# Two feature maps put behind the first residual adds, and LN1 statistics and token sums placed at other products of the first key/value groups

## The chip, the cores and the metric

The kernel runs on one core of one Trainium2 chip. The metric is the device time of one execution in microseconds (us), as the median of several executions. TensorE, VectorE, ScalarE and GpSimd are called PE, DVE, ACT and POOL in the profile; PEld are the weight loads of PE, SP is the engine that issues most DMAs.

## The reference, cut to what matters

```python
def _A_ref(x, wqkv, wo):                       # x: layernorm of the input, 2048 tokens x 1024
    qkv = ...                                  # x @ wqkv, 32 heads of 32
    phi = lambda t: where(t > 0, t + 1, exp(t)) + 1e-6
    pq, pk = phi(q), phi(k)
    kv = einsum("bhsd,bhse->bhde", pk, v)      # summed over all tokens
    z = einsum("bhsd->bhd", pk)
    num = einsum("bhqd,bhde->bhqe", pq, kv)
    den = einsum("bhqd,bhd->bhq", pq, z)[..., None] + 1e-6
    return (num / den) @ wo
h  = x + _A_ref(layernorm(x), wqkv, wo)        # attention block
h2 = h + _B_ref(layernorm(h), ...)             # gated FFN, 3584 wide; not touched here
```

## The kernel before: the parts that matter

Tokens come in 16 tiles of 128. For each pair of tiles the kernel computes keys ("key group" p), then values for pair p+2 ("value group" p+2); later it computes queries in eight groups. Every such group makes a 2x2 block product from seven products instead of eight, as in Strassen's scheme. This needs sums of weights (`TWv`, `TWk`), sums of tokens (`Sx`, by `x_sums`) and copies of partial results from one PSUM bank to another (`ident_act`, on ACT; PSUM is the memory that the products are written to). A product is four matmuls of 128x512. At fixed points of a group ("hooks") other work is queued for DVE and ACT.

```python
def sgroup(pool, tok_major, X, SX, W, TW, e11, e12, e21, e22, name, hooks=(), isphi=True):
    ...
    prod(a, X(0, 0), W(0, 0), True, "P1")
    ident_act(bank(b), bank(a), ...)              # bank copy: P6 waits for it
    hook(1)
    prod(f, SX(2), TW(2), True, "P7")
    ident_act(s7, bank(f), ...)
    hook(2)
    prod(b, SX(1), TW(1), False, "P6")            # needs token sum 2 and the bank copy
    ident_act(bank(c), bank(b), ...)              # bank copy: P5 waits for it
    hook(3)
    prod(a, X(1, 0), W(1, 0), False, "P2")
    for f_ in e11(...): f_()                      # keys: exp on ACT, two DVE ops ("finish")
    hook(4)
    prod(c, SX(0), TW(0), False, "P5")
    ident_act(sc, bank(c), ...); s22 = e22(...); s22[0]()     # an add on DVE
    hook(5)
    prod(b, X(1, 1), TW(3), False, "P4")
    s21 = e21(...); s21[0]()                      # an add on DVE
    hook(6)
    for f_ in s22[1:2]: f_()                      # exp on ACT
    prod(c, SX(3), W(1, 1), False, "P3")
    s12 = list(e12(...)); s12.pop(0)()            # (keys and queries) exp on ACT
    pend[1] = list(s22[2:]) + s12 + list(s21[1:]) # the rest runs at hook 1 of the next group
    hook(7)
```

The statistics of LN1, the first layernorm, run on ACT for some tiles: a pass for the mean and a pass of squares, which can be split in two ("half-squares"). Both write sums into a slot `s1`, of which there are two, and a few tiny POOL operations follow before the tile can be normalized (DVE) and transposed into place by a DMA.

```python
def ln1_stats_act(st, split=False):
    k = len(ln1_a) % 2                            # slot: tiles 5, 6, 7, 9 take 0, 1, 0, 1
    ...
# first value pieces (cut): ... m6(); v_piece(3, 0); ...; q6(); v_piece(2, 1); ...
def k5():                                         # key group p
    if p + 2 < NP_: x_sums(p + 2, 0)
    if p == 0: m_, q0_, q_ = ln1_stats_act(B, True); m_(); sq.extend([q0_, q_])   # B = 2p + 7
    elif B < NST: late_q.pop(0)()
def k6():
    if p + 2 < NP_: x_sums(p + 2, 1)
def v2(): if sq: sq.pop(0)()                      # value group p + 2
def v3(): if sq: sq.pop(0)()
          # p == 0: x_sums(1); norm(6)     else: norm(2 * p + 6)
def v5(): norm(2 * p + 7)
          # B = 2p + 9: m_, q0_, q_ = ln1_stats_act(B, True); m_(); q0_(); late_q.append(q_)
```

The output projection follows the last query group. Each pass multiplies tile t-4 by `wo` into one of two bank pairs, makes the next numerators, divides them (DVE), adds the residual of tile t-4 (`a4_h`, DVE, reads the bank pair) and takes its LN2 statistics on ACT, whose unused output goes to a scratch tile that shares memory with the exponentials.

```python
flush()                                           # the pending rest of the last query group
for t in range(NE, NST + LAG + 1):                # NE = LAG = 4
    if LAG <= t < NST + LAG: a4_mm(t - LAG)
    if t < NST: a2_num(t); a2_div(t)              # division, then a DMA transpose of the tile
    if LAG <= t < NST + LAG: a4_h(t - LAG)
    if LAG + 1 <= t < TPP + LAG + 1: a4_norm(t - LAG - 1)
    if t in (5, 7, 18, 19): load_w_next()         # 512 KB of FFN weights
    ...
```

## Time and profile before

| | before |
|---|---|
| median of executions | 723.82 us (723.69 to 724.08) |
| span of the profiled execution | 722.1 us, granted clock 0.999 |
| PE busy | 714.2 us (99%) |

The page of the kernel before: its span, the busy time of the engines, and the chain of waits by engine.

```profile
span 722.1 us, 12877 instructions
...
PE 714.2 (99%) x4905; PEld 380.4 (53%) x4905; DVE 587.5 (81%) x1024; ACT 359.2 (50%) x623; POOL 108.4 (15%) x177
...
PE 90%; DVE 6%; issue 1%; ACT 1%; POOL 1%; DMA 0%; ACTq 0%; DVEq 0%
```

PE is the limit, and the little that is not PE does not show in "99%". It shows in the timeline of PE. The columns are start, duration, engine, line, operation, tiles, matrix size, shape, number of merged instructions and, in brackets, the idle time before and what ended it. The first stretch is that of the early groups.

```profile
30.25 1.03 PE L766 MATMUL ps<-RW,RWG 128*128 128x512 f16 x4
31.69 1.02 PE L766 MATMUL ps<-RW,RWG 128*128 128x512 f16 x4 [0.41 <-DVE RWG L984]
32.55 1.03 PE L766 MATMUL ps<-RAB 128*128 128x512 bf16 x4
33.63 1.04 PE L766 MATMUL ps<-RW,RWG 128*128 128x512 f16 x4
...
35.47 0.70 PE L766 MATMUL ps<-RE 128*32 128x33 bf16 x64
...
37.84 1.03 PE L766 MATMUL ps<-RC,RWG 128*128 128x512 f16 x4
39.39 1.04 PE L766 MATMUL ps<-RC,RWG 128*128 128x512 f16 x4 [0.53 <-ACT ps L771]
```

Read starts here, not durations: a product of four lasts 1.03 us in the records and yet the next one starts 0.87 us later when nothing is in the way (the Trainium skill, Perfetto Trace Analysis, section Tensor Engine Instruction, says that the profiler works out a matmul's end rather than seeing it; this trace can't show that, but its records do overlap, 1.03 against 0.87). So between 30.25 and 31.69 there are 1.44 us where 0.87 are needed: a gap of 0.58 us, although the bracket has only 0.41. "Gap" below is always this: start to start, less the back-to-back time of the matmuls between. 33.63 has 0.22 and 39.39 has 0.69.

Why 39.39 is late stands in the timeline of ACT. L804 are statistics, L771 is the bank copy for which PE waits.

```profile
36.95 1.06 ACT L804 ACTIVATE RXH<-RE 128x1024 bf16<-128x1024 bf16 x1 [1.58 <-DVE RXH L890]
37.91 0.18 ACT L804 ACTIVATION_READ_ACCUMULATOR RXH<-RE 128x1 f32 x1
38.13 0.63 ACT L804 ACTIVATE RXH<-RE 128x512 bf16<-128x512 bf16 x1
38.67 0.19 ACT L804 ACTIVATION_READ_ACCUMULATOR RXH<-RE 128x1 f32 x1
38.76 0.58 ACT L771 ACTIVATE ps<-ps 128x512 f32<-128x512 f32 x1
```

ACT had idled 1.58 us for norm 6 (L890), which still read the statistics slot that tile 9's mean was to overwrite, and the copy then stood behind mean and half-square.

The fourth gap is in the projection. First PE, then DVE, in the kernel before:

```profile
174.71 0.37 PE L766 MATMUL ps<-kvz,RAB 32*128 32x33 bf16 x32
175.79 3.63 PE L766 MATMUL ps<-RW,RE 128*128 128x512 bf16 x16 [0.70 <-DVE RXH L1229]
```

```profile
171.77 0.28 DVE L849 TENSOR_SCALAR RX<-RX 128x512 bf16<-128x512 bf16 x1
172.09 0.69 DVE L852 SCALAR_TENSOR_TENSOR RAB<-RXH,RX 128x512 bf16<-128x512 f32 x1
172.70 0.18 DVE L1200 TENSOR_SCALAR dtmp<-ps 128x32 f32<-128x32 f32 x1
...
174.52 1.22 DVE L1229 TENSOR_TENSOR RXH<-ps,RC 128x1024 bf16<-128x1024 f32 x1
```

The third projection tile starts 1.08 us after the numerators, 0.77 more than the 0.31 of later tiles: it waits for the first residual add (L1229), in front of which DVE works off the finishes of the last query group (L849 and L852).

### The profile page before, as it was taken

How to read it: one execution, taken by the hardware profiler on the slowest of the kernel's cores; microseconds unless marked ns; L12 is line 12 of the kernel's file. 1: busy time of each engine (PE TensorE's matmuls, PEld its weight loads, DVE VectorE, ACT ScalarE, POOL GpSimd, SP SyncE). 2: the span in 40 equal slices, each digit the busy share in tenths (PEclk: the TensorE clock that was granted, in tenths of full speed). 3: DMA queues.
4: the chain of work that ended last, by engine and by line, in shares of the span. 5: the costliest groups of instructions: out<-in, count | busy, mean ns of one | idle time of the engine just before them, and what ended most of it. 6: DMA issues, size and time to landing. Idle time of an engine off the chain costs nothing.

```text
span 722.1 us, 12877 instructions
## 1 busy us (share of the span) xinstructions
PE 714.2 (99%) x4905; PEld 380.4 (53%) x4905; DVE 587.5 (81%) x1024; ACT 359.2 (50%) x623; POOL 108.4 (15%) x177
## 2 busy tenths in 40 slices
PE   8999999999999999999999999999999999999998
PEld 3444444444444444444444558865555545447887
DVE  7878867898775889889988787887889877887984
ACT  4877666764842456677756111035455545423010
POOL 2311100000360103332321001310000000000331
PEclk9999999999999999999999999999999999999999
DMA  9643245023998797999999989993564572037996
GB/s 310 214 98 80 44 126 163 6 30 72 211 221 262 230 282 236 273 302 312 298 273 275 310 251 322 319 208 114 149 172 135 161 250 78 1 102 249 323 315 178
DMA packets 192989, 143.64 MB, mean 199 GB/s; under 512 B 51872, under 2 KB 170400, under 8 KB 192928
## 3 DMA queue, kind: packets, MB, share of 16 engines
q1 hardware_dynamic: 188224, 138.50, 65.3%
q0 software_dynamic: 4032, 3.67, 3.5%
q8 instruction: 38, 0.62, 0.3%
q10 hardware_dynamic: 672, 0.66, 0.3%
q14 instruction: 23, 0.19, 0.1%
HBM read 98.76 MB, written 32.51 MB: 182 GB/s over the span
## 4 chain that ended last, share of the span: by engine, by line
PE 90%; DVE 6%; issue 1%; ACT 1%; POOL 1%; DMA 0%; ACTq 0%; DVEq 0%
PE ps L766 90%; DVE RAB L852 1%; DVE RE L1205 1%; DVE st L780 1%; DVE RX L849 1%; POOL rstd L790 0%; DVE RW L959 0%; DMA RE<-in_A_x_dram 0%; DVE RC L959 0%; DVE RX L1065 0%; ACT RX L845 0%; ACT RXH L804 0%; DVE RXH L834 0%; DVE rden L1203 0%; ACT ps L771 0%
## 5 line engine op out<-in xcount | busy, mean ns | idle before, releaser
L771 ACT ACTIVATE ps<-ps 128x512 f32<-128x512 f32 (+1 forms) x192 | 108.8, 567 | 217.4 <-PE ps L766 207.1
L766 PE MATMUL ps<-RC,RO 128*128 128x512 f16 x616 | 143.0, 369 | 0.0
L766 PE MATMUL ps<-RH,RWG 128*128 128x512 bf16 x448 | 108.1, 379 | 0.0
L766 PEld LDWEIGHTS ps<-RC,RO 128*128 128x128 f16 x616 | 60.3, 98 | 63.5
L766 PE MATMUL ps<-RC,RWG 128*128 128x512 f16 x320 | 76.7, 379 | 0.5 <-ACT ps L771 0.5
L766 PEld LDWEIGHTS ps<-RH,RWG 128*128 128x128 bf16 x448 | 43.8, 98 | 46.9
L1447 DVE TENSOR_TENSOR RAB<-ps,RAB 128x512 bf16<-128x512 f32 x56 | 37.3, 686 | 31.3 <-PE ps L766 31.3
L766 PE MATMUL ps<-RH,RO 128*128 128x512 bf16 (+1 forms) x256 | 61.2, 379 | 0.0
L766 PE MATMUL ps<-RW,RE 128*128 128x512 bf16 x256 | 57.6, 380 | 0.7 <-DVE RXH L1229 0.7
L1647 POOL DMA_DIRECT2D out_dram<-RX x20 | 17.9, 1257 | 263.3 <-DVE RX L1638 221.0
L766 PE MATMUL ps<-RAB 128*128 128x512 bf16 (+2 forms) x270 | 57.1, 351 | 0.1
L766 PE MATMUL ps<-RW,RAB 128*128 128x256 f16 (+3 forms) x362 | 52.9, 301 | 0.0
L766 PEld LDWEIGHTS ps<-RC,RWG 128*128 128x128 bf16 (+1 forms) x320 | 30.1, 98 | 40.1 <-ACT ps L771 6.1
L771 ACT ACTIVATE RE<-ps 128x512 f32<-128x512 f32 (+1 forms) x64 | 31.5, 502 | 37.8 <-PE ps L766 37.8
L766 PEld LDWEIGHTS ps<-RW,RAB 128*128 128x128 f16 (+1 forms) x362 | 35.4, 98 | 14.5
L1638 DVE TENSOR_TENSOR RE<-ps,RE 128x512 f32<-128x512 f32 x44 | 30.2, 687 | 14.3 <-PE ps L766 13.8
L771 ACT ACTIVATE RAB<-ps 128x512 bf16<-128x512 f32 x56 | 33.3, 595 | 16.5 <-PE ps L766 16.2
L1331 DVE TENSOR_TENSOR RO<-RWG 128x1024 f16<-128x1024 bf16 x54 | 36.9, 684 | 4.9 <-DMA RWG<-in_B_W_up_dram 4.9
L766 PEld LDWEIGHTS ps<-RH,RO 128*128 128x128 f16 (+1 forms) x256 | 24.4, 98 | 29.9 <-ACT RX L771 1.5
L1442 ACT ACTIVATE RAB<-RAB 128x1024 bf16<-128x1024 bf16 x28 | 29.5, 1055 | 19.5 <-DVE RAB L1433 19.0
L766 PEld LDWEIGHTS ps<-RW,RE 128*128 128x128 bf16 x256 | 24.0, 98 | 28.7 <-DVE RXH L1229 1.2
L766 PEld LDWEIGHTS ps<-RAB 128*128 128x128 bf16 (+1 forms) x270 | 26.0, 98 | 24.4 <-ACT RAB L908 1.0
(163 smaller groups left out, 1169.6 us busy)
## 6 DMA issues: line engine op xcount, KB each, us to landing
RWG<-in_B_W_gate_dram SPq DMA_DIRECT2D x28, 512.0 KB, 6.2
RWG<-in_B_W_up_dram SPq DMA_DIRECT2D x28, 512.0 KB, 5.2
RW<-l_scr SPq DMA_DIRECT2D x20, 448.0 KB, 5.6
RW<-in_B_W_down_dram SPq DMA_DIRECT2D x14, 512.0 KB, 5.2
t_scr<-RW SPq DMA_DIRECT2D x14, 512.0 KB, 4.9
l_scr<-RX SPq DMA_DIRECT2D x7, 1024.0 KB, 6.5
RE<-l_scr SPq DMA_DIRECT2D x15, 448.0 KB, 4.9
RE<-in_A_x_dram SPq DMA_DIRECT2D x23, 256.0 KB, 3.8
```

The source lines that it names most:

```text
L766: lambda e: e.matmul(out_ap, lhsT, rhs, start=start, stop=stop, skip_group_check=skip),
L771: PL.add("act", lambda e: e.activation(out=dst, in_=src, func=func), reads=reads, writes=writes, name=name)
L780: PL.add("dve", lambda e: e.bn_stats(out=st6[:, k, c * 6:(c + 1) * 6], in_=src_full[:, c * BCH:(c + 1) * BCH]), reads=[src_chunk_bufs[c]], ...
L849: PL.add("dve", lambda e: e.tensor_scalar(out=Et[:, k, :], in0=Et[:, k, :], scalar1=1.0, scalar2=1e-6, op0=ALU.min, op1=ALU.add), reads=[] ...
L852: PL.add("dve", lambda e: e.scalar_tensor_tensor(out=dst_ap, in0=src, scalar=C1, in1=Et[:, k, :], op0=ALU.add, op1=ALU.max), reads=[src_bu ...
L1205: PL.add("dve", lambda e: e.tensor_tensor(out=osb[:, k, :].rearrange("p (g h e) -> p g h e", h=HPG, e=Dh), in0=nv[:, :, :, 0:Dh], in1=rden ...
L1331: PL.add(eng, lambda e: e.tensor_tensor(out=tb(j, u), in0=f0(u), in1=f1(u), op=ALU.subtract), reads=[B_w[i + x] for x in r] + ([B_T[k + x] ...
L1442: PL.add("act", lambda e: e.activation(out=d, in_=d, func=ACTF.Relu), reads=[], writes=db, name=name)
L1447: PL.add("dve", lambda e: e.tensor_tensor(out=d, in0=bank(b), in1=d, op=ALU.mult), reads=[B_bank[b]], writes=[db], name=name)
L1638: PL.add(eng, lambda e: e.tensor_tensor(out=dst, in0=in0, in1=in1, op=op), reads=reads, writes=writes, name=name)
L1647: PL.add("pool", lambda e: e.dma_start(dst, src, accum_op=ALU.add), reads=[bsrc], writes=[B_hscr[st]], slot=sl, name="acc_%d_%d" % (st, dh))
```

## The change

Its intent: take DVE work from in front of the first residual adds, and place statistics and sums of the first groups so that PE's products are not kept waiting. The core of the diff:

```diff
-        s1 = sb("s1", [P, 2, 4], f32)
+        s1 = sb("s1", [P, 3, 4], f32)             # and k = len(ln1_a) % 3
 # sgroup, last query group
+            if last:
+                pend[1] = s12 + [s21[1]]
+                return [s22[2], s21[2]]           # two finishes, run by the caller
 # a4_h: scratch of the LN2 statistics
-            for f_ in act_stats(src, [B_hs[hs]], junk, B_junk, ...):
+            for f_ in act_stats(src, [B_hs[hs]], xn[:, st % NXN, :], B_xn[st % NXN], ...):
 # first value pieces
-        m6()
         v_piece(3, 0)
+        m6()
 ...
-        q6()
         v_piece(2, 1)
+        q6()
 ...
-        twv.pop(0)()                              # one of four value-weight sums; now in k6
 # key group p
+            def k4():
+                if p == 0: x_sums(2, 0)
             def k5():
+                if p == 0: x_sums(2, 1)
+                elif p + 2 < NP_: x_sums(p + 2, 0)
                 ...
-                elif B < NST: late_q.pop(0)()
+                while p > 0 and late_q: late_q.pop(0)()
             def k6():
+                if p == 0: twv.pop(0)()
 # value group p + 2
-                def v2(): ... sq.pop(0)()         # tile 7's half-squares now at v3 and v4
 # v3: norm(6) ahead of x_sums(1) when p == 0; from p = 1 on the first half-square of
 #     tile 2p + 9 moves from v5 to v3
                 def v5():
                     norm(2 * p + 7)
+                    if p == 0:
+                        m_, q0_, q_ = ln1_stats_act(9, True)
+                        m_(); late_q.extend([q0_, q_])
 # projection loop
                 a4_h(t - LAG)
+                run(late_phi, 1)
```

The scratch had to move with the late finishes: the old one shares memory with exponentials that they still read (so the code says).

More of the change, by code (lines that the diff above doesn't have):

```diff
@@ L321, in bass_sequential_preLN__linear_attn_block__glu_gated_reglu__prompt_kernel @@
         Et = RX[:, 0:NPH * NW].rearrange("p (a b) -> p a b", a=NPH)
-        ajunk = RX[:, 0:D]
         btmp = RX[:, NPH * NW:(NPH + 4) * NW].bitcast(f32).rearrange("p (a b) -> p a b", a=2)
@@ L427, in bass_sequential_preLN__linear_attn_block__glu_gated_reglu__prompt_kernel @@
         B_s2 = [bufs("s2_%d_" % i, 5) for i in range(2)]
-        B_s1 = [bufs("s1_%d_" % i, 4) for i in range(2)]
-        B_junk = _Buf("junk")
+        B_s1 = [bufs("s1_%d_" % i, 4) for i in range(3)]
         B_hnT = bufs("hnT_", TPP)
@@ L506, in bass_sequential_preLN__linear_attn_block__glu_gated_reglu__prompt_kernel @@
             b_.over = B_xn + B_hs
-        B_junk.over = B_E
         for b_ in flat(B_lsum):
-            b_.over = B_E + B_bt + [B_TWq[2], B_junk]
+            b_.over = B_E + B_bt + [B_TWq[2]]
         for b_ in B_hres + B_ds:
@@ L512, in bass_sequential_preLN__linear_attn_block__glu_gated_reglu__prompt_kernel @@
         for b_ in B_outst:
-            b_.over = B_E + B_bt + [B_TWq[2], B_junk]
+            b_.over = B_E + B_bt + [B_TWq[2]]
         for b_ in B_hnE:
@@ L880, in ln1_stats_act @@
             i = st % NX1
-            k = len(ln1_a) % 2
+            k = len(ln1_a) % 3
             ln1_a[st] = k
@@ L993, in x_sums, with sgroup @@
             add(3, xb(1, 0), s(1), ALU.subtract, [B_Sx[1][p]] + bx(1, 0))
-        def sgroup(pool, tok_major, X, SX, W, TW, e11, e12, e21, e22, name, hooks=(), isphi=True):
+        def sgroup(pool, tok_major, X, SX, W, TW, e11, e12, e21, e22, name, hooks=(), isphi=True, last=False):
             hooks = dict(hooks)
@@ L1157, in pl @@
                 return lambda b, bb: phi_steps(b, bb, d, db, "q_%d_%d" % (r, ct))
-            sgroup(A_POOL[r], False, X, SX, W, TW, pl(0, 0), pl(0, 1),
+            return sgroup(A_POOL[r], False, X, SX, W, TW, pl(0, 0), pl(0, 1),
                    add_phi(*dst(1, 0), "q_%d_%d" % (r, ct)),
-                   add_phi(*dst(1, 1), "q_%d_%d" % (r, ct)), "q%d%d" % (r, ct), hooks)
+                   add_phi(*dst(1, 1), "q_%d_%d" % (r, ct)), "q%d%d" % (r, ct), hooks,
+                   last=(r, ct) == (1, NG // 2 - 1))
         def kvacc(st):
@@ L1240, in a4_h @@
             src = hsb[:, hs, :]
-            junk = ajunk
-            for f_ in act_stats(src, [B_hs[hs]], junk, B_junk, s2[:, ks, 0:4], B_s2[ks], "ln2_%d" % st):
+            for f_ in act_stats(src, [B_hs[hs]], xn[:, st % NXN, :], B_xn[st % NXN], s2[:, ks, 0:4], B_s2[ks],
+                                "ln2_%d" % st):
                 f_()
@@ L1934, in bass_sequential_preLN__linear_attn_block__glu_gated_reglu__prompt_kernel @@
         m6, q6 = ln1_stats_act(6)
+        v_piece(3, 0)
         m6()
-        v_piece(3, 0)
         ln1_norm(5)
@@ L1939, in bass_sequential_preLN__linear_attn_block__glu_gated_reglu__prompt_kernel @@
         twk.pop(0)()
+        v_piece(2, 1)
         q6()
-        v_piece(2, 1)
         twv.pop(0)()
         twk.pop(0)()
-        twv.pop(0)()
         twv.pop(0)()
@@ L1960, in k1 @@
                     twq.pop(0)()
+            def k4():
+                if p == 0:
+                    x_sums(2, 0)
             def k5():
-                if p + 2 < NP_:
+                if p == 0:
+                    x_sums(2, 1)
+                elif p + 2 < NP_:
                     x_sums(p + 2, 0)
@@ L1968, in k5 @@
                     sq.extend([q0_, q_])
-                elif B < NST:
+                while p > 0 and late_q:
                     late_q.pop(0)()
             def k6():
-                if p + 2 < NP_:
+                if p == 0:
+                    twv.pop(0)()
+                elif p + 2 < NP_:
                     x_sums(p + 2, 1)
-            return {1: k1, 5: k5, 6: k6}, sq
+            return {1: k1, 4: k4, 5: k5, 6: k6}, sq
         def norm(st):
@@ L1998, in bass_sequential_preLN__linear_attn_block__glu_gated_reglu__prompt_kernel, with v3 @@
             if p + 2 < NP_:
-                def v2(sq=sq):
-                    if sq:
-                        sq.pop(0)()
-                def v3(p=p, sq=sq):
+                late = []
+                def v3(p=p, sq=sq, late=late):
                     if sq:
@@ L2006, in v3, with v4, v5 @@
                     if p == 0:
+                        norm(6)
                         x_sums(1)
-                        norm(6)
                     else:
                         norm(2 * p + 6)
-                def v5(p=p):
+                        if 2 * p + 9 < NST:
+                            m_, q0_, q_ = ln1_stats_act(2 * p + 9, True)
+                            q0_()
+                            late += [m_, q_]
+                def v4(sq=sq):
+                    if sq:
+                        sq.pop(0)()
+                def v5(p=p, late=late):
                     norm(2 * p + 7)
-                    B = 2 * p + 9
-                    if B < NST:
-                        m_, q0_, q_ = ln1_stats_act(B, True)
-                        m_()
-                        q0_()
-                        late_q.append(q_)
+                    if p == 0:
+                        m_, q0_, q_ = ln1_stats_act(9, True)
+                        m_()
+                        late_q.extend([q0_, q_])
+                    elif late:
+                        late[0]()
+                        late_q.append(late[1])
                 def v6(p=p, nq=nq):
@@ L2024, in v6 @@
                         twq.pop(0)()
-                v_group(p + 2, {2: v2, 3: v3, 5: v5, 6: v6})
+                v_group(p + 2, {3: v3, 4: v4, 5: v5, 6: v6})
         assert not twq and not twv and not twk
@@ L2038, in bass_sequential_preLN__linear_attn_block__glu_gated_reglu__prompt_kernel @@
                     hooks[6] = lambda t=ct: a2_num(t)
-                q_group(r, ct, hooks)
+                late_phi = q_group(r, ct, hooks)
                 if r == 1:
```

## The prediction

> **What bounds the kernel.** TensorE: matmuls busy 714.2 of 722.1 us (99%, page), granted clock 0.999, 90% of the chain of waits. The Trainium skill (Perfetto Trace Analysis, Identifying the Most-Contended Engine) warns that pipelined matmul busy time judges badly, so I measured in the timeline from matmul start to matmul start. A product of four 128x512 matmuls takes 0.87 us back to back. Beyond that, and 0.1 us per change of shape, four gaps lie where the change acts:
>
> - 31.69 us: 0.58 us, product 6 (P6) of value group 2: its token sum (VectorE, to 31.54) and bank copy (ScalarE, to 31.46) are late.
> - 33.63: 0.22 us, P5 there: its bank copy (32.98) stands behind a half-square of LN1 statistics (32.37).
> - 39.39: 0.69 us, P6 of key group 1: its bank copy (38.76) stands behind tile 9's mean (36.95, held until norm 6 by a shared statistics slot) and half-square (38.13).
> - 175.79: 0.86 us (0.77 net): the third output-projection tile waits for the first residual add (VectorE, 174.52 to 175.74), which reads the same banks.
>
> Sum 2.26 of 724 us. After 218 us no gap exceeds 0.25.
>
> **What the change does.**
>
> (a) The last query group's two feature-map finishes (0.92 us each) leave VectorE's queue ahead of the first residual add and run behind the first and second. VectorE runs without a pause from 163 to 178, so tile 4's division starts when its matmuls end (about 171.3) instead of 172.70, and the first add ends about 174.3, before 174.95 where its product could start. Later tiles have VectorE slack (idle 1.41 and 0.82). Gain 0.77.
>
> (b) The last value-weight sum (1.13 us) moves behind key group 0's feature maps, token sums of pair 2 one product earlier. The first finish starts near 27.6 instead of 28.21, the second token sum ends near 30.3 instead of 31.54. Then the bank copy rules; the exponentials ahead of it start 0.3 us earlier, so P6 starts near 31.2, 0.1 us late. Gain 0.45.
>
> (c) Tile 7's half-squares sit one product later, behind the copy; but the exponential ahead now waits for an add behind three token sums. Gain 0.15 to 0.2.
>
> (d) A third statistics slot frees tile 9's mean from norm 6; its half-squares go to the next group. Mean done near 36.4, copy on time near 37.4. Gain 0.65 to 0.7.
>
> (e) The new LN2 scratch tile: off the chain, zero.
>
> Against this, VectorE's backlog moves about 1 us later at 36 to 44 us, and two half-squares precede two exponentials in key group 1: a new gap of 0 to 0.2 us near value group 3.
>
> 2.26 less 0.2 to 0.3 left or new: 2.0 us. What follows is TensorE bound, so it should reach the end whole.
>
> **Predicted: 721.8 us, 8 in 10 within 721.2 to 723.0.** Faster by over 2%: 1%; within 2%: 98%; slower by over 2%: 1%.
>
> **Right or wrong shows in** the timeline: third output-projection tile 0.3 us after the division matmuls' start, not 1.08; key group 1's P6 without its 1.02 us weight-load wait on ScalarE; value group 2's P6 gap at most 0.2; TensorE's 0.7 us wait for the residual add gone.
>
> **Wrong if** the VectorE backlog holds token sums of pairs 1 or 3 (value group 3 waits over 0.3 us), if transposes of tiles 6 and 7 land later, if the late finishes delay later adds, or if the end hangs on a DMA that does not move along.

## The result, and the profile after

| | before | changed | |
|---|---|---|---|
| median | 723.86 us (723.69 to 724.08, 4 runs) | 722.61 us (722.40 to 723.35, 4 runs) | ratio 0.9984, 95% interval 0.9967 to 1.0002 |
| the same again, other chip | 724.49 us (9 runs) | 722.91 us (5 runs) | ratio 0.9981, 0.9967 to 0.9994 |
| span of the profiled execution | 722.1 us | 721.0 us; again 720.8 us | |

A ratio is the mean time of one kernel's fast runs over that of the other's of the same rounds, so not quite the ratio of the medians beside it. All runs told here are fast but one single run, whose state is unknown; their clocks lie between 0.999 and 1.0. The medians differ by 1.25 us, 0.17%. The first interval still includes 1, the second just does not: the gain is real by the second, and its size is loose. The page of the changed kernel:

```profile
span 721.0 us, 12872 instructions
...
PE 714.9 (99%) x4905; PEld 380.3 (53%) x4905; DVE 588.1 (82%) x1024; ACT 358.2 (50%) x623; POOL 110.7 (15%) x177
...
PE 94%; DVE 2%; DMA 2%; issue 1%; ACT 1%; POOL 0%; SPq 0%; DVEq 0%; ACTq 0%
```

The busy times do not tell that it is faster. PE's share of the chain went from 90 to 94%. The timeline of PE in the early groups (these line numbers are smaller by three in the changed kernel, so L763 is the L766 of before; of the later ones, the residual add L1229 is L1230):

```profile
30.20 2.06 PE L763 MATMUL ps<-RW,RWG 128*128 128x512 f16 x8
32.10 1.03 PE L763 MATMUL ps<-RAB 128*128 128x512 bf16 x4
33.07 1.04 PE L763 MATMUL ps<-RW,RWG 128*128 128x512 f16 x4
...
34.91 0.83 PE L763 MATMUL ps<-RE 128*32 128x33 bf16 x64
...
37.41 1.94 PE L763 MATMUL ps<-RC,RWG 128*128 128x512 f16 x8
...
43.59 1.03 PE L763 MATMUL ps<-RW,RWG 128*128 128x512 f16 x4
44.93 1.02 PE L763 MATMUL ps<-RW,RWG 128*128 128x512 f16 x4 [0.31 <-DVE RWG L981]
```

The three gaps have shrunk: P7 and P6 of value group 2 are now merged into one line of eight (0.16 us is left inside), P5 at 33.07 has 0.12, and in key group 1 P7 and P6 are one line too (nothing over the usual 0.04). But there are two new ones. The 64 small matmuls of the first key/value accumulation last 0.83 instead of 0.70, with a pause of 0.23 us in their middle (they follow each other faster than the spacing I reckon with, so of the pause 0.13 us are lost: the next product starts 0.76 us after the first of them, not 0.64), and at 44.93, P6 of value group 3, there are 0.48 us where before there were 0.04. What ACT and what DVE do ahead of 44.93:

```profile
41.69 0.62 ACT L801 ACTIVATE RXH<-RE 128x512 bf16<-128x512 bf16 x1
...
42.44 0.63 ACT L801 ACTIVATE RXH<-RE 128x512 bf16<-128x512 bf16 x1
...
43.06 0.61 ACT L842 ACTIVATE RX<-RX 128x512 bf16<-128x512 f32 x1
43.58 0.58 ACT L842 ACTIVATE RX<-ps 128x512 bf16<-128x512 f32 x1
44.06 0.59 ACT L768 ACTIVATE ps<-ps 128x512 f32<-128x512 f32 x1
```

```profile
31.30 1.22 DVE L956 TENSOR_TENSOR RW<-RAB,RW 128x2048 f16<-128x2048 bf16 x1
...
42.96 0.43 DVE L981 TENSOR_TENSOR RWG<-RAB 128x512 f16<-128x512 bf16 x1 [0.45 <-DMA RAB<-RXH]
...
44.35 0.42 DVE L981 TENSOR_TENSOR RWG<-RWG,RAB 128x512 f16<-128x512 f16 x1
```

The bank copy (L768) ends at 44.65, behind two half-squares (L801) and two exponentials. The token sum that P6 needs ends later still, at 44.77, because DVE stood 0.45 us for the transpose of tile 7. Which of them is the cause cannot be read from one trace. The 1.22 us weight sum (L956) is the piece that moved into DVE's queue here.

The projection, PE and DVE:

```profile
174.18 0.37 PE L763 MATMUL ps<-kvz,RAB 32*128 32x33 bf16 x32
174.49 3.63 PE L763 MATMUL ps<-RW,RE 128*128 128x512 bf16 x16
...
201.24 0.37 PE L763 MATMUL ps<-kvz,RAB 32*128 32x33 bf16 x32
201.80 3.61 PE L763 MATMUL ps<-RW,RE 128*128 128x512 bf16 x16 [0.19 <-DMA RE<-RE]
```

```profile
170.88 0.19 DVE L1201 TENSOR_SCALAR dtmp<-ps 128x32 f32<-128x32 f32 x1 [0.49 <-PE ps L763]
...
172.70 1.22 DVE L1230 TENSOR_TENSOR RXH<-ps,RC 128x1024 bf16<-128x1024 f32 x1
173.84 0.28 DVE L846 TENSOR_SCALAR RX<-RX 128x512 bf16<-128x512 bf16 x1
```

The third tile starts 0.31 us after the numerators, like all others: the gap is gone. DVE now waits for PE at 170.88, the add runs at 172.70, the first late finish (L846) after it. But at 201.80 the tenth tile starts 0.56 us after its numerators, 0.26 more than usual, for a DMA: the transposed tile landed at 201.7.

The stages, from the start of one matmul to the start of another (the same ones in all kernels, numbered in PE's order: 32, 361, 1301, 1471, 1901). Stage 1 is the value pieces and the early groups, stage 2 most of the rest of keys, values and queries, stage 3 the last query group and the first projection tiles, stage 4 most of the projection. From the end of stage 4 to the end of the span, which is nearly all FFN, it took 510.4 us in every trace of the tables.

| us | stage 1 | stage 2 | stage 3 | stage 4 |
|---|---|---|---|---|
| before | 43.48 | 107.15 | 17.52 | 34.34 |
| changed | 43.04 | 107.28 | 16.76 | 34.59 |
| changed, again | 42.78 | 107.25 | 16.75 | 34.53 |

Stage 3 gave what was forecast. Stage 1 gave 0.4 to 0.7 where 1.2 were gained at the three gaps, and stages 2 and 4 cost 0.1 and 0.2 to 0.25. Ahead of stage 1, where the change has no part, the traces differ as well: stage 1 starts at 9.16 us before, at 8.93 and 9.09 in the two of the changed kernel. So 0.23 and 0.07 us of the shorter spans are not the change's.

### The profile page after: what moved, and what is told of

Its sections match the earlier page's. It is cut to its first block, busy times and chain, and to the rows that moved or that the text cites. A ratio compares the mean times of both kernels' runs of the same rounds, so it can differ in the third digit from the quotient of the medians.

```text
span 721.0 us, 12872 instructions
## 1 busy us (share of the span) xinstructions
PE 714.9 (99%) x4905; PEld 380.3 (53%) x4905; DVE 588.1 (82%) x1024; ACT 358.2 (50%) x623; POOL 110.7 (15%) x177
## 4 chain that ended last, share of the span: by engine, by line
PE 94%; DVE 2%; DMA 2%; issue 1%; ACT 1%; POOL 0%; SPq 0%; DVEq 0%; ACTq 0%
PE ps L763 94%; DMA RE<-RE 1%; DMA RAB<-RXH 1%; DVE RWG L981 0%; DMA RE<-in_A_x_dram 0%; ACT RXH L801 0%; PE ps L902 0%; DVE RX L1065 0%; DVE RE L1639 0%; DVE st L777 0%; DVE RXH L1230 0%; DVE RE L1126 0%; ACT RXH L1256 0%; DVE RW L956 0%; DVE RX L846 0%
## 5 line engine op out<-in xcount | busy, mean ns | idle before, releaser
L768 ACT ACTIVATE ps<-ps 128x512 f32<-128x512 f32 (+1 forms) x192 | 108.9, 567 | 221.5 <-PE ps L763 214.7
L763 PE MATMUL ps<-RC,RO 128*128 128x512 f16 x616 | 143.0, 369 | 0.0
L763 PE MATMUL ps<-RH,RWG 128*128 128x512 bf16 x448 | 108.1, 379 | 0.0
L763 PEld LDWEIGHTS ps<-RC,RO 128*128 128x128 f16 x616 | 60.3, 98 | 63.5
L763 PE MATMUL ps<-RC,RWG 128*128 128x512 f16 x320 | 76.8, 379 | 0.0
L763 PEld LDWEIGHTS ps<-RH,RWG 128*128 128x128 bf16 x448 | 43.8, 98 | 46.9
L763 PE MATMUL ps<-RH,RO 128*128 128x512 bf16 (+1 forms) x256 | 61.2, 379 | 0.0
L763 PE MATMUL ps<-RW,RE 128*128 128x512 bf16 x256 | 57.6, 379 | 0.2 <-DMA RE<-RE 0.2
L763 PE MATMUL ps<-RAB 128*128 128x512 bf16 (+2 forms) x270 | 57.1, 351 | 0.1
L763 PE MATMUL ps<-RW,RAB 128*128 128x256 f16 (+3 forms) x362 | 52.9, 301 | 0.0
L763 PEld LDWEIGHTS ps<-RC,RWG 128*128 128x128 bf16 (+1 forms) x320 | 30.0, 98 | 39.8 <-ACT ps L768 5.8
L768 ACT ACTIVATE RE<-ps 128x512 f32<-128x512 f32 (+1 forms) x64 | 31.5, 503 | 37.8 <-PE ps L763 37.8
L763 PEld LDWEIGHTS ps<-RW,RAB 128*128 128x128 f16 (+1 forms) x362 | 35.3, 98 | 14.5
L768 ACT ACTIVATE RAB<-ps 128x512 bf16<-128x512 f32 x56 | 33.3, 594 | 16.9 <-PE ps L763 16.5
L763 PEld LDWEIGHTS ps<-RH,RO 128*128 128x128 f16 (+1 forms) x256 | 24.4, 98 | 29.9 <-ACT RX L768 1.5
L1434 DVE TENSOR_TENSOR RAB<-ps,RE 128x512 bf16<-128x512 f32 x56 | 37.2, 685 | 2.2 <-PE ps L763 1.9
L763 PEld LDWEIGHTS ps<-RAB 128*128 128x128 bf16 (+1 forms) x270 | 26.0, 98 | 24.4 <-ACT RAB L905 1.1
```

The costliest lines, as they stand in the source:

```text
L763: lambda e: e.matmul(out_ap, lhsT, rhs, start=start, stop=stop, skip_group_check=skip),
L768: PL.add("act", lambda e: e.activation(out=dst, in_=src, func=func), reads=reads, writes=writes, name=name)
L1434: PL.add("dve", lambda e: e.tensor_tensor(out=d, in0=src, in1=ftmp[:, u, :], op=ALU.add), reads=[bsrc, B_s5[u]], writes=[db], name=name)
```

## The experiments

Twelve runs, on four chips, each batch beside runs of the kernel before on its own chip. Four of the traces that the stages are read from lack 56 of 4905 matmul records; I matched the rest by their order. My theory was that each gap acts by itself, that gains and new gaps add up, and that the new gap at 44.93 comes from DVE's longer queue through the late transpose. Rivals: the new gaps are chance of one execution; the half-squares on ACT make them; the early gain is given back later.

### late_only, front_only: the two halves of the change

`late_only` is the kernel before with the late finishes and the new scratch; `front_only` is the changed kernel without them.

```diff
 # late_only, against before
+            if last: pend[1] = s12 + [s21[1]]; return [s22[2], s21[2]]
+                run(late_phi, 1)                  # after a4_h; and scratch xn[:, st % NXN, :]
 # front_only, against the changed kernel: these three edits taken out, the scratch left
```

Expected of `late_only`:

> Part (a) alone on the kernel before: the two late feature-map finishes with the new LN2 scratch tile. Theory: the parts add up, and this one removes only the gap in front of the third output-projection tile (0.86 to 0.09 us), so 0.77 us: 723.1 us, and the three early gaps (0.58, 0.22, 0.69 us) stay as in the kernel before. Rival: the gap is given back later (the finishes delay tiles 5 to 7, or the end hangs on something else), then the matmul starts after 190 us, or the total, move less than 0.5 us.

Expected of `front_only`:

> The whole change without part (a). Theory: the three early gaps shrink from 1.49 to about 0.3 us, but the change opens new ones in the same stage: 0.4 to 0.5 us at product 6 of value group 3 (its token sum waits for tile 7's transpose, which VectorE's backlog sends off late) and 0.1 to 0.2 us inside the first kv accumulation; net gain 0.4 to 0.6 us, 723.3 us; the gap at 175 us stays at 0.86. Rival: the new gap at value group 3 was a chance lateness of one transfer in one execution; then it is under 0.1 us here and the gain is about 1.0 us.

| | time (before 723.76) | ratio | stage 1 | stage 2 | stage 3 | stage 4 |
|---|---|---|---|---|---|---|
| late_only | 723.39 us | 0.9996 (0.9984 to 1.0009) | 43.60 | 107.15 | 16.75 | 34.40 |
| front_only | 723.47 us | 0.9997 (0.9984 to 1.0009) | 42.70 | 107.25 | 17.52 | 34.36 |

Stage 3 moves by 0.77 us with the late finishes and by nothing without them. That settles part (a). The time of `late_only` moved only 0.37 us; in its trace stage 4 took 0.06 more and its early stage had a gap of 0.80 us of another kind, told below. The three early gaps did not stay as expected either (0.03, 0.38 and 0.44 us instead of 0.58, 0.22 and 0.69; more under `slot_late`). So its expected total was missed. In `front_only` the new gap at P6 of value group 3 came back with 0.25 us instead of 0.48, and the pause in the first accumulation with 0.23. So they are not chance, but half of the first was.

### slot_only, slot_late: one line, and one line with part (a)

```diff
-        s1 = sb("s1", [P, 2, 4], f32)
+        s1 = sb("s1", [P, 3, 4], f32)             # and % 3; slot_late adds the edits of late_only
```

> The kernel before with three LN1 statistics slots instead of two, nothing else. Theory: tile 9's mean no longer waits for norm 6 and both its mean and its half-square end by 37.2 us, so the bank copy of key group 1 is on time: the 0.69 us gap is gone, the 0.58 and 0.22 us gaps stay, and no new gap over 0.1 us comes at value group 3 (its token sum would end 0.1 to 0.2 us before it is needed): 723.2 us, a larger gain than all of the early part of the change. Rival: any kernel in which TensorE runs ahead here meets the late transpose of tile 7, so value group 3 waits 0.4 us or more here too and the gain is under 0.4 us.

> Part (a) and the third statistics slot on the kernel before, nothing else. Theory: gains add, 0.77 and 0.69: 722.4 us, the same as or 0.1 to 0.3 us under the whole change, although it leaves the gaps of 0.58 and 0.22 us in value group 2. Rival: the reorderings of sums and statistics pay on balance, then this is at least 0.4 us slower than the whole change (723.0 us).

| | time (before 723.76) | ratio | stage 1 | stage 2 | stage 3 | stage 4 |
|---|---|---|---|---|---|---|
| slot_only | 723.45 us | 0.9996 (0.9982 to 1.0009) | 43.70 | 107.16 | 17.52 | 34.37 |
| slot_late | 722.83 us | 0.9989 (0.9976 to 1.0001) | 42.79 | 107.16 | 16.75 | 34.73 |

In both traces the 0.69 us gap of key group 1 is gone, and value group 3 has no gap over 0.04 us: the third slot alone takes the first away and opens no second. The gain in time, 0.31 us, was half of what was expected.

Both expectations said that the gaps of 0.58 and 0.22 us in value group 2 would stay. They did not. PE in `slot_late`:

```profile
30.67 1.93 PE L763 MATMUL ps<-RW,RWG 128*128 128x512 f16 x8
...
33.68 1.04 PE L763 MATMUL ps<-RW,RWG 128*128 128x512 f16 x4 [0.22 <-ACT ps L768]
```

P7 and P6 are one line (0.03 us), and P5 has 0.38; `slot_only` and `late_only` have the same. Nothing in these kernels mends P6. PE came to P7 at 30.67, 31.29 and 31.02 us, late by gaps further ahead, where it came at 30.25 in the kernel before; the token sum ended at 31.39, 31.96 and 31.69, against 31.54 there, in time for a PE that is late. So value group 2 lost 0.41 us in these three traces, not 0.80: the gap of 0.58 us was seen only where PE came early (there, and as 0.63 in `tw_back`, at 30.35), and gaps do not simply add up.

The two traces also say why one profile proves little here: the code of stage 1 is the same in both, and stage 1 differs by 0.9 us, through gaps of 0.61 and 0.68 us at 18 and 26 us in `slot_only` against one of 0.40 at 18 in `slot_late`. `slot_late` has the worst stage 4 of these four, with 0.26 us at the tenth tile and 0.15 at the ninth. Whether it equals the whole change is not settled: 0.9989 against 0.9984 and 0.9981 on other chips, inside the intervals.

### after_again, q0_back, tw_half, w_early: which new gap has which cause

`after_again` is the changed kernel unedited. The others each undo or mend one thing in it:

```diff
 # q0_back: tile 9's first half-square back in value group 2
-                        m_(); late_q.extend([q0_, q_])
+                        m_(); q0_(); late_q.append(q_)
 # tw_half: the moved weight sum in two halves, the first ahead of the first finish
+            def k3():
+                if p == 0: tw4.pop(0)()           # half the rows; k6 runs the other half
 # w_early: FFN weight loads ahead of the projection loop
+        load_w_next(); load_w_next()
-            if t in (5, 7, 18, 19):
+            if t in (18, 19):
```

> The changed kernel once more, unedited, to tell chance from cause. Theory: the new gaps of its first profile come from its order and return: at product 6 of value group 3 (0.48 us then) at least 0.2 us, inside the first kv accumulation 0.2 to 0.25 us; the wait of the projection for a transposed tile near 202 us (0.26 us beyond the usual 0.09) may move between 0 and 0.3 us, because its transfer takes 3.3 to 5 us. Rival: they were chance, and under 0.1 us here. Time 722.4 to 722.9 us.

> The changed kernel with tile 9's first half-square back in value group 2, where ScalarE idles 1.4 us. Theory: at product 6 of value group 3 ScalarE's copy comes about 0.6 us earlier, but the gap there stays at 0.3 to 0.5 us, because VectorE's token sum, which waits for tile 7's transpose, ends last; no gain on its own (0 to 0.1 us). Rival: ScalarE's two half-squares in key group 1 make the gap; then it is under 0.1 us and the gain 0.4 us.

> The changed kernel with the moved weight sum cut into two halves: the first fills VectorE's 0.78 us pause before the first feature-map finish (about 26.8 to 27.4 us), the second stays behind. Theory: VectorE's backlog shrinks by about 0.55 us: the gap in the first kv accumulation (0.24) goes, norms 6 and 7 come 0.5 us earlier, tile 7's transpose lands 0.3 to 0.5 us earlier, and the gap at product 6 of value group 3 falls from 0.48 to about 0.25 us, where ScalarE's copy is then last: gain 0.4 us, 722.2 us. Rival: the transposes are held by their own queue, not by VectorE, and land when they did: only the 0.24 us go.

> The changed kernel with the first two FFN weight loads (512 KB each) issued before the projection loop instead of in it (there they are issued near 183 and 192 us, between transposes). Theory: in the projection the transposes of the output tiles 6 to 9 land 0.5 to 2 us earlier, each with over 1 us to spare, and no projection tile waits for one: the gap near 202 us falls to 0.09 us; gain 0.2 to 0.3 us if that gap is there without the edit. Rival: the transposes slow each other, not the loads; then landing times and the gap stay as they are.

Gaps in us; the last two columns are the transpose of the tenth tile of the projection from issue to landing, and PE's gap before that tile beyond the usual 0.09.

| | time (before 724.49) | value group 3, P6 | pause, first accumulation | transpose, tenth tile | gap, tenth tile |
|---|---|---|---|---|---|
| after_again | 722.91 us | 0.25 | 0.23 | 5.0 | 0.19 |
| q0_back | 722.64 us | 0.04 | 0.24 | 4.8 | 0.09 |
| tw_half | 722.32 us | 0.26 | none | 3.4 | none |
| w_early | 722.81 us | 0.26 | 0.23 | 3.1 | none |

Ratios to before were 0.9981, 0.9979, 0.9975 and 0.9979, all with intervals of about 0.0013 either way, so the times do not part these kernels; the gaps do.

The gap at value group 3 was where I erred. I expected it to stay in `q0_back`, and it went. The trace of `q0_back`, PE first (P7 and P6 are one line of eight), then ACT:

```profile
43.97 1.93 PE L763 MATMUL ps<-RW,RWG 128*128 128x512 f16 x8
```

```profile
42.08 0.62 ACT L801 ACTIVATE RXH<-RE 128x512 bf16<-128x512 bf16 x1
...
42.94 0.63 ACT L842 ACTIVATE RX<-RX 128x512 bf16<-128x512 f32 x1
43.48 0.58 ACT L842 ACTIVATE RX<-ps 128x512 bf16<-128x512 f32 x1
44.23 0.58 ACT L768 ACTIVATE ps<-ps 128x512 f32<-128x512 f32 x1 [0.18 <-PE ps L763]
```

With one half-square ahead of the exponentials, the bank copy waits for PE and not PE for it. So 0.25 us of this gap belongs to the half-square that the change moved into key group 1. PE came to this group 0.27 us later here than in `after_again`, held by a gap of 0.81 us at 18 us, and that alone could have hidden the gap. `best1` below settles it: PE comes 0.14 us earlier than in `after_again`, and with the half-square back there is still only 0.03. The other 0.2 in the first profile came on top, in an execution where tile 7's transpose landed at 42.9; where DVE did not have to wait for it (`after_again`, 42.5) the gap was 0.25. `m6_again`, told below, repeats the larger gap: the transpose landed at 43.4, DVE stood 0.42 us for it, and P6 had 0.47.

`tw_half` shows that the pause in the first accumulation is the moved weight sum: with half of it in DVE's idle time it is gone. (The gap at value group 3, which was to fall from 0.48 to 0.25, says nothing here: `after_again` has 0.25 too.) `w_early` shows the loads' part in the projection: without them between the transposes, the eighth, ninth and tenth tile landed 3.0, 3.7 and 4.1 us ahead of their products, against 1.9, 0.5 and 0.1 us in `after_again`; in `best1`, with the same edit, it was 2.7, 3.6 and 4.1. In the traces with the loads in place the tenth transpose took either 3.1 to 3.4 us or 4.6 to 5.0 us; only in the second case, and only with part (a) in, did PE wait over 0.05 us for it (0.06 to 0.43 us). `tw_half` and `m6_old` had no wait with the loads in place, so for the wait itself the two traces with the loads moved are few.

### best1, tw_back, m6_old

`best1` has all three repairs. `tw_back` undoes the move of the weight sum, `m6_old` that of tile 6's statistics in the first value pieces.

```diff
 # tw_back
+        twv.pop(0)()                              # before v_piece(3, 1), and none in k6
 # m6_old
+        m6()
         v_piece(3, 0)
-        m6()
 ...
+        q6()
         v_piece(2, 1)
-        q6()
```

> The changed kernel with the three repairs that the runs so far point to, together: tile 9's first half-square back in value group 2, the moved weight sum cut in two halves, and the first two FFN weight loads ahead of the projection loop. Theory: each takes away a gap of its own, and they add up: at product 6 of value group 3 from 0.25 to under 0.1 us, in the first kv accumulation from 0.23 to 0, near 202 us to 0.09; together 0.45 to 0.7 us under the changed kernel. Rival: with those gaps gone TensorE runs into the next wait in the same places and less than 0.3 us is left.

> The changed kernel with the last value-weight sum back ahead of key group 0's feature maps, the token sums left at their new products. Theory: the gap at product 6 of value group 2 (0.16 us) grows to 0.5 to 0.7 us, because the first finish and the adds behind it, and with them ScalarE's exponentials and its bank copy, come 0.6 us later; the gap of 0.23 us in the first kv accumulation goes, for VectorE's queue is shorter there. Net loss 0.2 to 0.4 us in the early stage against the changed kernel. Rival: the earlier token sums alone keep product 6 on time; then its gap stays under 0.2 us and the kernel gains 0.2 us.

> The changed kernel with tile 6's two statistics passes back ahead of the value copies in the first value pieces. Theory: where the load of tile 6's tokens lands late (21 us and more instead of 20) ScalarE waits in the mean, its value copies and the bank copy of key group 0 come late, and TensorE has a gap of 0.5 to 0.8 us at product 6 of key group 0 near 25 us, as two of the four profiles with the old order had (0.80, 0.68 us; the other two none) and none of the new order over 0.2. Then the gap at product 6 of value group 2 closes. On time 0 to 0.4 us slower. Rival: the old order is no worse; that gap is under 0.2 us although the load lands after 21 us.

| | time (before 723.93) | ratio | stage 1 | stage 2 | stage 3 | stage 4 |
|---|---|---|---|---|---|---|
| best1 | 722.49 us (722.34 to 722.55) | 0.9978 (0.9965 to 0.9990) | 42.45 | 107.53 | 16.75 | 34.35 |
| tw_back | 722.83 us | 0.9984 (0.9972 to 0.9997) | 43.09 | 107.25 | 16.76 | 34.80 |
| m6_old | 723.95 us (722.76 to 724.42) | 1.0001 (0.9987 to 1.0014) | 42.68 | 107.56 | 16.76 | 34.35 |

In `best1` all three are gone; its stage 1 is the shortest of all, its stage 4 as short as any with part (a). Its stage 2 has 0.28 us at one product near 104 us, which `q0_back` and `m6_old` have too and the changed kernel does not; I did not find out why. In time it lies 0.0003 to 0.0006 under the changed kernel in ratio, 0.2 to 0.4 us, on another chip and inside the intervals: better than the changed kernel is not shown, and the 0.45 to 0.7 us expected were missed.

In `tw_back` PE's timeline has the gap back at P6 of value group 2, now with ACT's copy as the one waited for:

```profile
30.35 1.03 PE L763 MATMUL ps<-RW,RWG 128*128 128x512 f16 x4
31.84 1.04 PE L763 MATMUL ps<-RW,RWG 128*128 128x512 f16 x4 [0.47 <-ACT ps L768]
```

That is 0.63 us against 0.16, and the pause in the first accumulation is gone, as expected. So, in an execution in which PE comes as early as here, moving the weight sum gains 0.47 and costs 0.13, and moving the token sums alone would not have done. (Its stage 4 is the longest: 0.43 us at the tenth tile, the chance of this execution.)

`m6_old` is the surprise: an edit that only swaps statistics and copies in the first value pieces leaves four of five executions 1.1 to 1.7 us slower than the fifth, on which its profile fell, and slower than all of `best1` and `tw_back` on the same chip. What may lie behind it is seen in `late_only`, which has the old order. ACT, then PE:

```profile
21.59 1.06 ACT L801 ACTIVATE RXH<-RE 128x1024 bf16<-128x1024 bf16 x1 [1.14 <-DMA RE<-in_A_x_dram]
...
25.12 0.60 ACT L768 ACTIVATE ps<-ps 128x512 f32<-128x512 f32 x1
```

```profile
25.79 1.04 PE L763 MATMUL ps<-RC,RWG 128*128 128x512 f16 x4 [0.63 <-ACT ps L768]
```

ACT stands 1.14 us at the mean of tile 6, whose tokens landed at 21.5 us; everything queued behind it, down to the bank copy of key group 0, is late, and PE has a gap of 0.80 us. The Trainium skill (PSUM — Partial Sum Buffer, section Engine vs sequencer instructions) calls ScalarE's queue strictly first in, first out, and this trace agrees: a value copy that had its product stood behind the mean and ran at 22.65, where in the changed kernel, with the mean behind it, it ran at 20.27. In the profile of the kernel before the load landed at 20.0 and nothing of this was to be seen.

### m6_again

The same kernel as `m6_old`, for a second profile.

> The kernel of the last run with tile 6's statistics in the old order, unedited, for a second profile: its first profile fell on its fastest execution (722.76 us; tile 6's tokens landed at 20.2 us), the other four took 723.8 to 724.4 us. Theory: with a load landing after 21 us this profile has a gap of 0.5 to 0.8 us at product 6 of key group 0 near 25 us that the changed kernel does not have (0.25 at most), and the span is 0.5 us or more over the first profile's. If the load lands near 20 us again, it shows no such gap and nothing is settled. Rival: the load lands late, but the gap is under 0.3 us; then the slow executions have another cause.

Its time was 723.48 us in a single execution (state unknown), its span 721.7 us, 0.7 over the first profile (0.3 of it a single gap at 221 us, which no other trace has). The load landed at 21.2, ACT stood 0.71 us for it, and P6 of key group 0 had a gap of 0.43 us: between the two theories' numbers. In the changed order, with loads landing at 21.2 to 21.4, it was 0.13, 0.18, 0.25 and 0.19 us in four traces and none in two, in which PE was already late from a gap at 18 us. So in these traces the reordering saves 0.2 to 0.3 us when the load is late. That does not explain executions of 724.3 us; their cause is open. The old order alone does not bring them: `slot_late` has it too, and its five executions took 722.7 to 723.5 us.

## Why the prediction was right or wrong

The time was predicted as 721.8 us within 721.2 to 723.0, and came out at 722.61: inside, but 1.25 us of gain instead of 2.0. Its own sign of being wrong, value group 3 waiting over 0.3 us, came true in the first profile (0.48) and in `m6_again` (0.47), and not in the other traces of the changed order.

- **Part (a), gain 0.77: right.** Stage 3 went from 17.52 to 16.76 us, and with part (a) alone to 16.75. The add, forecast to end at 174.3, ended at 173.9. The late finishes held up no later add.
- **Part (b), gain 0.45: right beside the one profile it was read from.** The gap went from 0.58 to 0.16, gain 0.42; the first finish started at 27.58 (forecast 27.6), the token sum ended at 30.32 (30.3), P6 started at 31.22 (31.2). `tw_back` shows that the weight sum's move is what does it. But three other traces of the old order have no such gap (0.03), since PE comes later there; value group 2 lost 0.41 us in them and 0.27 in the changed kernel.
- **Part (c), gain 0.15 to 0.2: a little less.** 0.22 to 0.12.
- **Part (d), gain 0.65 to 0.7: right.** 0.69 to under 0.04; `slot_only` shows that the third slot does it alone. The other half of (d), moving tile 9's first half-square into key group 1, was allowed 0 to 0.2 us and cost more (next point).
- **The failed term: "2.26 less 0.2 to 0.3 left or new".** The four gaps gave 1.96 us (0.77, 0.42, 0.11, 0.66); what was new measured 1.1 us in the first profile (0.44, 0.26, 0.13, 0.13, 0.10, and 0.07 at 18 us) and 0.8 in the second (0.22, 0.19, 0.18, 0.13, 0.10). So the four waits were right and this term was mis-sized: 1.1 to 1.4 us left or new, where 0.2 to 0.3 were forecast. For value group 3 the prediction had "0 to 0.2 us": it was 0.25, from ACT's half-squares, plus 0.2 more in one execution from the late transpose. Three costs were not in it at all: 0.13 us in the first accumulation, from the backlog it had itself named; 0.26 and 0.19 us at the tenth projection tile, a transposed tile landing too late for a PE that runs earlier; and 0.1 us in three later key groups (0.03 each, cause not sought). The reordered value pieces, left out of the sum, go with the 0.13 and 0.18 us at key group 0 where the profile before had none; but that was an execution with a timely load. The times of `m6_old` suggest that the reordering is worth more than it costs, which is not shown while their cause is open.
- **"It should reach the end whole": mostly.** What is left after the projection reaches the end (the rest takes 510.4 us whatever came before), but the projection itself takes part of it back, in executions where its transposes are slow. In the two traces with the weight loads moved ahead (`w_early`, `best1`) it does not.

## What to carry to other kernels

In this kernel, with PE busy 99% of the time, what was left were gaps of half a microsecond, and a bracket, a share or a busy time did not show their size: measure from start to start, and in more than one profile, for a gap can be there in one execution and be closed by an earlier gap in the next. Removing one makes PE arrive earlier everywhere behind it, so list for each later product how much time its other inputs had to spare, and expect every input with less slack than the gain to become the next wait, DMA landings included. And a queue that works in order should not hold a wait for a load ahead of work that is ready: one profile can show such a load on time and hide the cost.

## What the Trainium skill lacked or had wrong

- Perfetto Trace Analysis, Identifying the Most-Contended Engine: it names weight-load share and useful arithmetic as better measures than matmul busy time. Neither finds a loss of this size: weight loads were busy 380.4 us before and 380.3 us after, and the arithmetic is the same, while the span fell by 1.0 us.
- Perfetto Trace Analysis, Optimization Strategy: it looks for the gaps between slices. Here the slices of PE overlap, and the gap between them was 0.41 us where start to start gave 0.58, and nothing where it gave 0.22 (33.63 us in the kernel before). The page times by start-to-start spacing for GpSimd alone.
- DMA: Bandwidth & Descriptors, DMA Transpose (X-bar): no time from issue to landing. Here a 128x1024 bf16 transpose within SBUF took 3.1 to 5.0 us for the same tile (the tenth of the projection) in different executions.
- ScalarE: Activation LUTs mentions the accumulator output, but no page has its cost: each accumulating activation is followed by an ACTIVATION_READ_ACCUMULATOR of 0.18 to 0.23 us, and a 512-wide half-square holds the queue for 0.61 us (32.37 to 32.98 in the kernel before) where a plain 512-wide copy holds it for about 0.5.
